# Deferred inverse transforms of eight token tiles, each issued four down matmuls later

## The chip, the cores and the metric

The kernel runs on one core of a Trainium2 chip. The metric is the device time in microseconds (us) of that core, as the median of several executions. A program on one core has no second core to compare its state with, so a run counts as undisturbed when the profile's granted TensorE clock is 1.000 and its time lies within 1.5% of the fastest of the same kernel. "Stage" means one stretch of a trace: from the end of the first block of gate/up matmuls to the start of the second. That is where the change acts.

## The reference

A layer on 2048 tokens of 576 features: a spectral filter (a 2D real FFT, a product with weights, the inverse FFT) added to the input, then a gated feed-forward part added to that.

```python
x = A_x
h = x + irfft2(rfft2(layernorm(x)) * (w_r + 1j * w_i))        # spectral part
n = layernorm(h)
h2 = h + (gelu(n @ w_gate) * (n @ w_up)) @ w_down             # 576 -> 4608 -> 576
```

## The kernel before

Almost all of the work is matmuls, the transforms too. (PSUM is the memory in which matmul results land, in banks; every matmul comes with a load of its weights, "PEld" in the traces.) The kernel has 16 token tiles of 128 tokens, and the feed-forward part goes in four blocks of four tiles: 36 groups of gate/up matmuls (each ends in a GELU on ScalarE and a product on VectorE), then the down matmuls. Only the first eight tiles have their last inverse transform done before the feed-forward part starts. The other eight are "deferred": their transforms are spread among the 288 down matmuls of the first block, whose own tiles don't need them.

A deferred tile has two parts. The first part is eight matmuls into PSUM banks 2 and 3, a ScalarE copy (EB) and four VectorE sums (two into QB, two into YB). The second part is two matmuls on YB into banks 4 and 5, an add onto the residual XO (VectorE) and a sum of squares (ScalarE).

```python
def def_i(c):                                   # "first part"
    ...                                         # 8 matmuls of 144 columns -> banks 2, 3      (L877)
    P.op(ACT, ... activation(EB, bank 2, Copy))                                             # (L880)
    for i, op in enumerate((ALU.add, ALU.subtract)):
        P.op(DVE, ... tensor_tensor(QB[i], bank 3, EB, op))                                 # (L884)
    P.op(DVE, ... tensor_tensor(y2[:, :, 0:HK], QB[:, 0::2, :], QB[:, 1::2, :], add))       # (L886)
    P.op(DVE, ... tensor_tensor(y2[:, ::-1, ...], QB..., QB..., subtract))                  # (L887)

def def_n(c):                                   # "second part"
    ...                                         # 2 matmuls of 288 columns on YB -> banks 4, 5 (L891)
    P.op(DVE, ... tensor_tensor(x2, banks 4 and 5, x2, add))                                # (L894)
    square(c, JD[:, :], "JD")                                                               # (L746)

DSTEP, DLAG = (36, 22) if NPRE == 8 else (28, 22)      # NPRE is 8
for j, c in enumerate(range(NPRE, NT)):
    defer(DSTEP * j, def_i, c)                  # before down matmul number 36 * j
    defer(DSTEP * j + DLAG, def_n, c)           # 22 down matmuls later

def down(tb, p):                                # one token tile, in two halves of 36 matmuls
    for h, (d0, d1) in enumerate(((0, cut), (cut, D))):
        for k, f in enumerate(...):
            if tb == 0:
                for fn in DEF.get(72 * p + 36 * h + k, ()):
                    fn()
            P.op(PE, ... matmul(bank b, AT[:, f, ...], WD[:, f, d0:d1]))                    # (L926)
        P.op(DVE, ... tensor_tensor(OS, bank b, XO, add))      # eviction of the half       # (L929)
```

In the traces here VectorE works in the order in which the program issued its instructions (in the first unit of the stage: lines L848, L884, L886, L887, L894, L929). So where a part is deferred to decides two things: how many down matmuls TensorE can do while VectorE works on the tile, and behind what the tile's VectorE work queues.

## Time and profile before

| kernel before | value |
|---|---|
| time, median of 3 runs (lowest to highest) | 492.3 us (492.15 to 492.36) |
| span of the profiled execution | 490.0 us |
| TensorE busy | 484.2 us, 99% |
| the stage | 129.98 to 171.35, 41.37 us |
| one deferred tile's cadence in it | 5.16 us |

The prediction shows the rows that carry this. One view it only mentions is the busy time of each engine in the stage's first two units. The columns are the stretch, its length, and for each engine the busy time and the number of instructions.

```profile
core 0: us, PE busy (x) PEld busy (x) DVE busy (x) ACT busy (x) POOL busy (x), PEclk, DMA share, GB/s
130.00:135.30 5.30, 5.30 (x50) 4.27 (x51) 3.54 (x7) 1.77 (x4) 0.00 (x0) 1.00 0.02 3
135.30:140.40 5.10, 5.10 (x49) 4.16 (x47) 2.86 (x6) 1.28 (x3) 0.00 (x0) 1.00 0.05 14
```

TensorE (PE) is busy without a gap. VectorE (DVE) works 2.86 us in a usual unit, and 3.54 us in the first, which still has the last product of the gate/up block to do. That product is what the first tile's sums queue behind: they start 1.34 us after the tile's first part (129.98 to 131.32), against 0.73 us in the next unit (135.26 to 135.99).

### The profile page before, as it was taken

The page shows a single profiled execution, that of the slowest core. Times are in us where ns is not written, and L with a number is a line of the kernel's source. Part 1 is how long each engine was busy: PE and PEld are TensorE (multiplying, and loading weights), DVE is VectorE, ACT ScalarE, POOL GpSimd, SP SyncE. Part 2 cuts the span into 40 slices and gives each one's busy share as a digit, 9 for nine tenths or more (in the row PEclk, how much of TensorE's full clock was granted, in tenths as well). Part 3 has the DMA queues.
Part 4 walks back from the last instruction along what each step waited for, and adds up shares of the span by engine and source line. Part 5 has one row for each costly group of instructions (what it writes and reads, how often), then busy time and mean ns, then how long its engine had stood idle before and what let it go on. Part 6 is the DMA issues. An engine that isn't in the chain of part 4 may idle for free.

```text
span 490.0 us, 9898 instructions
## 1 busy us (share of the span) xinstructions
PE 484.2 (99%) x4373; PEld 285.7 (58%) x4374; DVE 190.9 (39%) x381; ACT 150.9 (31%) x291; POOL 33.4 (7%) x61
## 2 busy tenths in 40 slices
PE   7999999999999999999999999999999999999998
PEld 3787754444588744444577644444677544444775
DVE  6999623443455534333311144433211233333111
ACT  6899852233222222322200033233100122323000
POOL 6411541000000020000000000000000000000000
PEclk9999999999999999999999999999999999999999
DMA  8990997211000071100000001000000000000000
GB/s 281 242 324 18 373 372 272 70 25 21 1 14 17 13 233 23 23 4 1 1 18 14 19 18 23 17 0 1 7 19 19 7 0 1 1 1 1 14 19 18
DMA packets 25147, 31.26 MB, mean 64 GB/s; under 512 B 11440, under 2 KB 17840, under 8 KB 25104
## 3 DMA queue, kind: packets, MB, share of 16 engines
q1 hardware_dynamic: 22208, 18.68, 13.1%
q0 software_dynamic: 2896, 11.95, 6.9%
q8 instruction: 34, 0.56, 0.5%
q14 instruction: 9, 0.07, 0.1%
HBM read 26.29 MB, written 2.36 MB: 58 GB/s over the span
## 4 chain that ended last, share of the span: by engine, by line
PE 96%; DVE 1%; DMA 1%; SPq 0%; POOL 0%; issue 0%; POOLq 0%; DVEq 0%
PE PS L839 57%; PE PS L926 29%; PE PS L600 2%; PE PS L610 2%; PE PS L531 1%; PE PS L717 1%; DMA XO<-in_A_x_dram 1%; PE PS L640 1%; PE PS L755 1%; PE PS L877 1%; DVE ST L475 1%; PE PS L891 0%; PE PS L804 0%; SPq L221 0%; DVE VR L655 0%; DVE TP L619 0%
## 5 line engine op out<-in xcount | busy, mean ns | idle before, releaser
L839 PE MATMUL PS<-HT,WG 64*128 64x512 bf16 (+1 forms) x2142 | 228.5, 373 | 0.0
L839 PEld LDWEIGHTS PS<-HT,WG 64*128 64x128 bf16 x2142 | 104.1, 94 | 122.7 <-issue 0.7
L848 DVE TENSOR_TENSOR AT<-GL,PS 128x512 bf16<-128x512 bf16 x144 | 99.0, 688 | 177.5 <-ACT GL L847 177.5
L847 ACT ACTIVATE GL<-PS 128x512 bf16<-128x512 f32 x144 | 85.9, 597 | 262.4 <-PE PS L839 248.9
L926 PE MATMUL PS<-WD,AT 128*128 128x288 bf16 (+2 forms) x1152 | 144.3, 286 | 0.0
L926 PEld LDWEIGHTS PS<-WD,AT 128*128 128x128 bf16 x1152 | 110.7, 98 | 30.8 <-ACT GL L847 1.3
L929 DVE TENSOR_TENSOR OS<-PS,XO 128x288 bf16<-128x288 f32 (+2 forms) x32 | 14.6, 458 | 100.4 <-PE PS L926 100.4
L839 PE MATMUL PS<-HT,WGX 64*128 64x512 bf16 x486 | 53.4, 376 | 0.0
L839 PEld LDWEIGHTS PS<-HT,WGX 64*128 64x128 bf16 x486 | 23.7, 94 | 28.7
L746 ACT ACTIVATE JD<-XO,NM 128x576 bf16<-128x576 bf16 x8 | 6.2, 776 | 28.4 <-DVE XO L894 28.4
L600 PE MATMUL PS<-FT,U 128*128 128x288 bf16 x96 | 14.2, 287 | 0.0
L619 DVE TENSOR_TENSOR TP<-YS,WS 128x1152 bf16<-128x1152 bf16 (+2 forms) x17 | 11.8, 718 | 0.3
L531 PE MATMUL PS<-ATS,XO 128*128 128x128 bf16 (+1 forms) x128 | 10.1, 221 | 1.4 <-POOL XN L545 0.8
L475 DVE BATCH_NORM_STATS2 ST<-XO 128x6 f32<-128x288 bf16 x24 | 9.3, 438 | 4.1 <-DMA XO<-in_A_x_dram 4.1
L600 PEld LDWEIGHTS PS<-FT,U 128*128 128x128 bf16 x96 | 9.2, 98 | 2.4 <-DVE U L540 0.2
L591 ACT ACTIVATE YS<-PS 128x576 bf16<-128x576 f32 x15 | 9.6, 651 | 2.0 <-PE PS L610 1.8
L531 PEld LDWEIGHTS PS<-ATS,XO 128*128 128x128 bf16 (+1 forms) x128 | 7.4, 97 | 4.4 <-POOL XN L545 1.3
L610 PE MATMUL PS<-CUS,BT 128*128 128x288 bf16 x64 | 10.0, 286 | 0.0
L591 ACT ACTIVATE CUS<-PS 128x576 bf16<-128x576 f32 x14 | 9.1, 650 | 0.8 <-PE PS L600 0.4
L894 DVE TENSOR_TENSOR XO<-PS,XO 128x576 bf16<-128x576 f32 x8 | 6.1, 758 | 8.0 <-PE PS L891 8.0
L640 PE MATMUL PS<-VT,ZS 128*128 128x256 bf16 x64 | 8.8, 273 | 0.3 <-DVE ZS L630 0.3
L591 ACT ACTIVATE V<-PS 128x512 bf16<-128x512 f32 (+1 forms) x17 | 9.0, 582 | 0.0
(79 smaller groups left out, 210.2 us busy)
## 6 DMA issues: line engine op xcount, KB each, us to landing
WD<-in_B_w_down_dram POOLq DMA_DIRECT2D x9, 576.0 KB, 10.7
WG<-in_B_w_up_dram SPq DMA_DIRECT2D x4, 1152.0 KB, 6.9
WG<-in_B_w_gate_dram POOLq DMA_DIRECT2D x4, 1152.0 KB, 9.7
out_dram<-OS SPq DMA_DIRECT2D x30, 72.0 KB, 1.6
XO<-in_A_x_dram SPq DMA_DIRECT2D x3, 576.0 KB, 7.0
WGX<-in_B_w_up_dram SPq DMA_DIRECT2D x1, 1152.0 KB, 6.0
WGX<-in_B_w_gate_dram POOLq DMA_DIRECT2D x1, 1152.0 KB, 9.9
HT<-HN SPq DMA_TRANSPOSE x60, 2.4
```

The source lines that it names most:

```text
L475: P.op(DVE, lambda v, c=c, h=h: v.bn_stats(ST1[:, c, h, :], XO[:, c, 288 * h:288 * h + 288]), r=[("X", c)], w=[("ST1", c, h)])
L531: P.op(PE, lambda t, b=b, lhs=lhs, p0=p0, p1=p1, s=s, e=e, o=o, c=c: t.matmul(bank(b, p0, p1, o, o + 128), lhs, ATS[:, c, :], start=s, sto ...
L591: fn = (lambda v: v.tensor_copy(dst, src)) if eng == DVE else (lambda a: a.activation(dst, src, ACTF.Copy))
L600: P.op(PE, lambda t, b=b, m=m, us=us, o=o, g=g: t.matmul(bank(b, 0, 128, 0, 2 * HK), U[:, us, g, :, :], FT[:, 3 * o + (2 if us == 4 else u ...
L610: P.op(PE, lambda t, b=b, tb=tb, m=m, s3=s3, sp_=sp_: t.matmul(bank(b, 0, 128, 0, KW), BT[:, sp_, tb, :], CUS[:, s3, m, :], start=(m == 0) ...
L619: P.op(DVE, lambda v: v.tensor_tensor(TP[:, sl, :, :, q0:q1], y4, w4, op=ALU.mult), r=[("Y", sl), ("Wn", i)] + (wkeys[0] if 1 <= g < 9 els ...
L640: P.op(PE, lambda t, b=b[c], c=c, zp=zp, sp_=sp_, z3=z3: t.matmul(bank(b, 0, 128, 256 * c, 256 * c + 256), ZS[:, z3, zp, c:256:2], VT[:, s ...
L839: op = P.op(PE, lambda t, h0=h0, kt=kt, wt=wt, b=b, s=(not second and j == 0), e=(second and j == n - 1): t.matmul(bank(b, 0, 128, c0, c1) ...
L847: P.op(ACT, lambda a: a.activation(GL[:, s2, :], bank(b0), ACTF.Gelu_apprx_tanh), r=[("PS", b0)], w=[("GL", s2)])
L848: P.op(DVE, lambda v: v.tensor_tensor(AT[:, f, :], GL[:, s2, :], bank(b0 + 1), op=ALU.mult), r=[("GL", s2), ("PS", b0 + 1)], w=[("AT", f)])
L926: P.op(PE, lambda t, b=b, d0=d0, d1=d1, f=f, p=p: t.matmul(bank(b, 0, 128, 0, d1 - d0), AT[:, f, 128 * p:128 * p + 128], WD[:, f, d0:d1], ...
L929: P.op(DVE, lambda v, b=b, d0=d0, d1=d1, p=p, c=c: v.tensor_tensor(OS[:, p % 2, d0:d1], bank(b, 0, 128, 0, d1 - d0), XO[:, c, d0:d1], op=A ...
```

## The change

The intent, as I read it, is slack. Each deferred tile keeps its distance of 22 down matmuls between its parts, but both parts come four down matmuls later. So the first tile's VectorE work no longer meets the end of the gate/up block quite as closely.

```diff
     for j, c in enumerate(range(NPRE, NT)):
-        defer(DSTEP * j, def_i, c)
-        defer(DSTEP * j + DLAG, def_n, c)
+        defer(DSTEP * j + 4, def_i, c)
+        defer(DSTEP * j + DLAG + 4, def_n, c)
     if NPRE < 8:
         ...                                     # t2 gets + 4 too; not taken: NPRE is 8
```

More of the change, by code (lines that the diff above doesn't have):

```diff
@@ L907, in _build @@
     for j, c in enumerate(range(NPRE, NT)):
-        defer(DSTEP * j, def_i, c)
-        defer(DSTEP * j + DLAG, def_n, c)
+        defer(DSTEP * j + 4, def_i, c)
+        defer(DSTEP * j + DLAG + 4, def_n, c)
     if NPRE < 8:
-        t2 = DSTEP * (8 - NPRE) + DLAG
+        t2 = DSTEP * (8 - NPRE) + DLAG + 4
         defer(t2 - 14, ln2_late, 3)
```

## The prediction

> **What bounds the kernel now.** I read the page first, for which engine the span is made of:
>
> ```profile
> span 490.0 us, 9898 instructions
> ...
> PE 484.2 (99%) x4373; PEld 285.7 (58%) x4374; DVE 190.9 (39%) x381; ACT 150.9 (31%) x291; POOL 33.4 (7%) x61
> ...
> PE 96%; DVE 1%; DMA 1%; SPq 0%; POOL 0%; issue 0%; POOLq 0%; DVEq 0%
> ```
>
> TensorE is busy for 99% of the span, at a clock that is never throttled (the view of the cores gives a mean granted clock of 1.000), and 96% of the chain that ended last is TensorE. But the page says of itself that a busy TensorE is not one at its peak, so a waiting matmul could hide in that 99%. What counts is the cadence of the matmuls in the stage that the change touches. So the second view is that chain in order of time, around the first block of down matmuls (source line 926), where the eight deferred tiles are worked off: L877 is the first matmul group of a deferred inverse transform (eight matmuls, I call it "first part"), L891 the second (two matmuls, "second part"), L839 the gate/up matmuls on either side.
>
> ```profile
> 129.98 0.61 PE PS L877 x8
> 130.59 2.69 PE PS L926 x22
> 133.55 1.72 PE PS L926 x14
> 135.26 0.50 PE PS L877 x8
> 135.76 2.69 PE PS L926 x22
> 138.70 1.72 PE PS L926 x14
> ...
> 171.35 70.04 PE PS L839 x648
> 241.38 35.39 PE PS L926 x288
> ```
>
> The columns are start, duration (us), then engine, tile, line and count. The reader is to see a strict repeat. A unit is 8 first-part matmuls, 22 down, 2 second-part (0.24 to 0.26 us, too short to be listed here), 14 down, and the next unit starts 5.16 us later; there is no row of anything but TensorE between 129.98 and 171.35. Waits are the third view, limited to this stage. For TensorE itself it lists nothing, for its weight loads two rows, and the other engines wait for TensorE:
>
> ```profile
> DVE XO L894 <- PE PS L891: 8.0, 8, 1.1
> DVE OS L929 <- PE PS L926: 7.9, 8, 1.0
> ACT EB L880 <- PE PS L877: 2.1, 7, 0.3
> ...
> DVE QB L884 <- ACT EB L880: 1.4, 7, 0.2
> PEld PS L877 <- issue: 0.4, 1, 0.4
> PEld PS L839 <- issue: 0.2, 1, 0.2
> ```
>
> The two weight-load rows are the two changes of matmul kind at the stage's ends. They happen once each. So the stage runs at TensorE's rate, and everything on VectorE and ScalarE lies beside it.
>
> **What the Trainium skill says.** "TensorE: Matmul & The Clock Gate", section "Wait — 56ns, not 53.3ns?", gives for a warm stream a start-to-start of N / 2.4 GHz plus about 2.5 ns. Worked out (an estimate from that page): 122.5 ns for the 288 columns of a down or second-part matmul, 62.5 ns for the 144 columns of a first-part one. The trace agrees to the last digit it shows: 36 down matmuls in 2.69 + 1.72 = 4.41 us are 122.5 ns each, and eight first-part ones in 0.50 us are 62.5 ns each. So the formula is a usable zero line, and whatever a stage takes above it is what better placing could win. "PSUM — Partial Sum Buffer", section "PSUM bank collisions raise a hardware error", asks that PSUM be guarded by bank; this matters here because a moved matmul could be made to wait for a bank. By the source the down matmuls of this block use banks 0 and 1 (6 and 7 for the last tile), the first part 2 and 3, the second 4 and 5. The trace agrees that none is waited for: no TensorE wait row in the stage. "Trainium Architecture — The Big Picture", section "What this means for kernel authors", has the engines as independent processors that meet only at semaphores; the trace agrees, with TensorE continuous while VectorE works about 2.9 us of each 5.16 us unit.
>
> **The change part by part.** It removes nothing and adds nothing: same 288 down, 64 first-part and 16 second-part matmuls, same copies and adds. It moves every first part from just ahead of a half's first down matmul to after four of them, and every second part from after 22 to after 26. The 22 down matmuls between a tile's two parts stay 22. (The branch for fewer than eight early tiles isn't taken: the kernel has eight.)
>
> The ceiling of a gain. Zero line of the stage by the two rates: 288 x 122.5 ns + 64 x 62.5 ns + 16 x 122.5 ns = 35.28 + 4.00 + 1.96 = 41.24 us. Measured: 171.35 - 129.98 = 41.37 us. Only 0.13 us is there to be won. Of it 0.11 us is the first unit's first group, 0.61 us where the others take 0.50: the change from gate/up to full-height matmuls. The change keeps that, it only falls on a down matmul: where a later block goes from gate/up straight to down matmuls, its 288 take 35.39 us, that is 35.39 - 35.28 = 0.11 us over. That leaves 0.02 us, and it can be found. In the first unit L926 starts at 130.59 and resumes at 133.55, 2.96 us; in the next 135.76 to 138.70, 2.94 us. The detailed timeline says why:
>
> ```profile
> 130.58 0.41 ACT L880 ACTIVATE EB<-PS 128x288 f32<-128x288 f32 x1
> 130.72 0.69 DVE L848 TENSOR_TENSOR AT<-GL,PS 128x512 bf16<-128x512 bf16 x1 [0.18 <-ACT GL L847]
> 131.32 0.81 DVE L884 TENSOR_TENSOR QB<-PS,EB 128x288 f32<-128x288 f32 x2
> 132.17 0.46 DVE L886 TENSOR_TENSOR YB<-QB 128x288 bf16<-128x288 f32 x1
> 132.54 0.45 DVE L887 TENSOR_TENSOR YB<-QB 128x288 bf16<-128x288 f32 x1
> 133.11 0.13 PEld L891 LDWEIGHTS PS<-YB,ITD 128*128 128x128 bf16 x2
> ```
>
> The first tile's VectorE chain queues behind the last gate product (L848), ends at 132.99, and TensorE wants its result at 133.11: just in time. This is surely what the change is after. Four down matmuls (0.49 us) later, the chain still starts near 131.3 (it waits for that same product), so it ends near 133.0, while its user comes at about 133.6. Slack grows from about 0.1 to 0.6 us, and 0.02 us of time is won. For the seven other tiles the whole chain moves along with its own matmuls: in the last, L887 ends at 168.61 and the second part's load starts at 169.10, so its slack of about 0.5 us stays.
>
> Costs at the other end. The stage's last second part is followed by 10 down matmuls instead of 14, so its residual add (169.67 for 0.76 us), its square and the GpSimd statistics run 0.49 us later. The add would end at 170.92, still ahead of the last down eviction at 171.45. The statistics now end at 171.71 + 1.65 = 173.36, then at about 173.85; their first user, the normalisation of tile 8, starts at 177.69, after a gate product that it queues behind. The weights loaded into the space freed here are issued at 172.31 to 174.2 and land at most 10.4 us later; the first matmul to use them loads at 222.66. A slip of 0.5 us against 3.8 and 38 us costs nothing. Sum: -0.02 + 0 = -0.02 us, on 492.3.
>
> **The rivals.** First, that the move collides on VectorE: the eviction of a finished half (L929, 0.46 us at 135.30) ran between one tile's add and the next tile's first sum. In the changed order the add ends 0.49 us nearer to it (134.34 + 0.49 = 134.83, still 0.47 us before), and the next sum starts later (135.99 + 0.49), further from it. If they did collide, a tile's chain would slip by at most 0.46 us, against its slack of 0.5; even all eight going 0.1 us past it would cost 0.8 us, 0.2%. Second, that the move takes a real stall out of every half boundary, because a down bank or a deferred bank is held there. For: that is where the change is made. Against: the groups of eight take 0.50 us, which is exactly their rate, and the down groups too. It would need 1.2 us a boundary to make 2%, and the excess of the whole stage is 0.13 us. Third, that ScalarE delays the chain: its square (134.38 to 135.25) ends 0.30 us before the next tile's copy at 135.55; both shift together, so that gap stays. Fourth, a slip at the stage's end that delays the weight load of a later block: it would have to be 38 us.
>
> **Range and chances.** The prediction is the time before, 492.3 us, as 0.02 us is below its last digit. Three runs before spread over 0.2 us; a repetition, another instruction layout or a chip warmed otherwise may shift by about twice that, which is my choice for the range: 491.9 to 492.7. For a change of 2% (9.8 us) the eight units would each have to move by 1.2 us, a quarter of their length, and no rival comes near. I give 1% to either side for what I haven't seen.
>
> **What would show it right or wrong.** Right: from the end of the first gate/up block to the start of the second still 41.3 to 41.4 us; first groups of down matmuls now 4 then 22 then 10 long; first-part groups at 0.50 us, all of them; the extra 0.11 us now on the first four down matmuls (about 0.60 us); the second part's first load with an idle gap of nothing, and the VectorE chain of the first tile ending about 0.6 us before it; no TensorE wait row. Wrong: a row of VectorE or ScalarE in the chain between 130 and 172 us, a TensorE wait for YB, EB or an XO add, or units longer than 5.16 us. It would also be wrong by a clock granted below 1.0, which nothing here would cause.

## The result, and the profile after

The changed kernel takes 492.26 us (median of 6 runs, 492.17 to 492.33) beside 492.23 us for the kernel before (6 runs, 491.98 to 492.6); 492.3 was predicted. The ratio is 1.0, with a 95% interval of 0.9988 to 1.0013.

The whole page first: the profiled span is 490.2 us instead of 490.0.

```profile
span 490.2 us, 9899 instructions
...
PE 483.9 (99%) x4373; PEld 285.7 (58%) x4374; DVE 191.0 (39%) x381; ACT 151.0 (31%) x291; POOL 33.4 (7%) x61
```

The 0.2 us aren't the change's. The chain that ended last, in order of time, has its first large row here for the kernel before:

```profile
2.12 5.44 DMA XO<-in_A_x_dram
```

and here for the changed one:

```profile
2.12 5.61 DMA XO<-in_A_x_dram
```

The load of the input took 0.17 us longer in this execution, 120 us before the first changed instruction, and all that follows is late by it or by 0.02 us more. Comparing times of day between the two traces therefore needs an offset of 0.19 us at the stage's start (129.98 against 130.17). Durations need none. The same chain in the stage of the changed kernel:

```profile
130.17 0.60 PE PS L926 x4
130.77 0.50 PE PS L877 x8
131.27 2.69 PE PS L926 x22
...
134.21 1.72 PE PS L926 x14
135.92 0.50 PE PS L877 x8
136.42 2.69 PE PS L926 x22
...
170.29 1.23 PE PS L926 x10
171.52 70.04 PE PS L839 x648
```

The stage is 171.52 - 130.17 = 41.35 us, against 41.37: the 0.02 us that was forecast. The groups of 22, of 14 and of 8 take what they took. The first four down matmuls carry the 0.11 us for changing over from gate/up matmuls (0.60 us in place of 0.49), which the first eight L877 carried before. The last group of the stage is 10 long, as the second part moved toward the stage's end. The first unit in detail shows the slack:

```profile
130.90 0.69 DVE L848 TENSOR_TENSOR AT<-GL,PS 128x512 bf16<-128x512 bf16 x1 [0.17 <-ACT GL L847]
131.05 0.41 ACT L880 ACTIVATE EB<-PS 128x288 f32<-128x288 f32 x1 [0.18 <-PE PS L877]
131.50 0.82 DVE L884 TENSOR_TENSOR QB<-PS,EB 128x288 f32<-128x288 f32 x2
132.73 0.45 DVE L887 TENSOR_TENSOR YB<-QB 128x288 bf16<-128x288 f32 x1
133.68 0.22 PEld L891 LDWEIGHTS PS<-YB,ITD 128*128 128x128 bf16 x2
133.80 0.41 PE L891 MATMUL PS<-YB,ITD 128*128 128x288 bf16 x2
```

These are selected rows. The tile's first sum (L884) starts at 131.50, which is 1.33 us after the stage's start; before it was 131.32 - 129.98 = 1.34 us. The four down matmuls ahead of the first part have not delayed it, because it was waiting on VectorE for L848 anyway. They take up just that wait: the copy now ends at 131.05 + 0.41 = 131.46, 0.04 us before the first sum. Its last sum ends at 133.18, and the weight load of the second part comes at 133.68. Before, the two were at 132.99 and 133.11, with the load held back. The last tile's slack is 0.50 us as well (169.26 to 169.76), so the change has brought the first tile level with the others.

### The profile page after: what moved, and what is told of

Read it like the earlier page. It is cut to its first block, busy times and chain, and to the rows that moved or that the text cites. A ratio compares the mean times of both kernels' runs of the same rounds, so it can differ in the third digit from the quotient of the medians.

```text
span 490.2 us, 9899 instructions
## 1 busy us (share of the span) xinstructions
PE 483.9 (99%) x4373; PEld 285.7 (58%) x4374; DVE 191.0 (39%) x381; ACT 151.0 (31%) x291; POOL 33.4 (7%) x61
## 4 chain that ended last, share of the span: by engine, by line
PE 96%; DVE 1%; DMA 1%; SPq 0%; POOL 0%; issue 0%; POOLq 0%; DVEq 0%
PE PS L839 57%; PE PS L926 29%; PE PS L600 2%; PE PS L610 2%; PE PS L531 1%; PE PS L717 1%; DMA XO<-in_A_x_dram 1%; PE PS L640 1%; PE PS L755 1%; PE PS L877 1%; DVE ST L475 1%; PE PS L891 0%; PE PS L804 0%; SPq L221 0%; DVE VR L655 0%; DVE TP L619 0%
## 5 line engine op out<-in xcount | busy, mean ns | idle before, releaser
L848 DVE TENSOR_TENSOR AT<-GL,PS 128x512 bf16<-128x512 bf16 x144 | 99.0, 688 | 177.4 <-ACT GL L847 177.4
```

The source lines that it names most:

```text
L848: P.op(DVE, lambda v: v.tensor_tensor(AT[:, f, :], GL[:, s2, :], bank(b0 + 1), op=ALU.mult), r=[("GL", s2), ("PS", b0 + 1)], w=[("AT", f)])
```

## The experiments

Times with rounds come from two groups of four kernels, each with its own runs of the kernel before on the same chip: 492.16 us in the first group, 492.25 us in the second. In some of these traces the chain leaves TensorE in the first unit. There the stage's start is read as the start of the block's last GELU less 0.10 us, which is its place in the other traces (for example 130.27 against 130.17 in the changed kernel; 0.11 in the kernel before), so such a stage is good to about 0.01 us.

**How long may a tile take? The second parts sooner.** With the first parts as in the kernel before, the distance is 6 instead of 22. My theory is that TensorE sets the stage and placement is free as long as a tile's chain of sums ends in time; the rival is that chain or load give way.

```diff
-        defer(DSTEP * j + DLAG, def_n, c)
+        defer(DSTEP * j + 6, def_n, c)
```

> First parts as in the kernel before, second parts 6 down matmuls after them. My theory: a second part is due 1.24 us after the first part's start (1.35 in the first unit) but can run at 2.72 (3.31) us, so TensorE stalls 1.48 us in each of seven units and 1.96 us in the first: 12.3 us in all, stage about 53.6 us, time about 504.6 us, 2.5% slower. The rival that the chain gets shorter when TensorE is idle, or that the weight load ahead of the matmul hides more: less than 10 us.

It took 504.01 us, ratio 1.0239 (1.0224 to 1.0254). The chain in order of time, one unit in the middle and the end:

```profile
137.47 0.26 PE PS L877 x4
137.76 0.42 ACT EB L880
...
139.51 0.38 DVE YB L887
...
139.94 0.42 PE PS L891 x2
140.36 3.67 PE PS L926 x30
144.03 0.26 PE PS L877 x4
...
183.42 6.58 PE PS L839 x59
```

Now ScalarE and VectorE are in the chain: the tile's copy and sums set the cadence. The stage is 183.42 - 130.23 = 53.19 us, 11.82 us longer than that of the kernel before (12.3 was expected; the rival with less than 10 us is out), and the time is 11.85 us above the kernel before: what the stage loses, the kernel loses in full. A unit of the seven later ones takes (183.42 - 137.47) / 7 = 6.56 us, 1.41 us over 5.155 (36 + 2 matmuls of 122.5 ns and 8 of 62.5 ns), where 1.48 was expected. The second part was due 1.24 us after its first part's start, so it can run 1.24 + 1.41 = 2.65 us after it. With 22 it is due at 0.50 + 22 x 0.1225 = 3.20 us. **The reserve of the seven later units is 0.55 us**, some four and a half down matmuls.

**At the edge, with and without the moved first part.** The distance is 18 in both of these; in the second, the first parts stand four later, as in the change.

```diff
-        defer(DSTEP * j, def_i, c)
-        defer(DSTEP * j + DLAG, def_n, c)
+        defer(DSTEP * j + 0, def_i, c)          # the other kernel: + 4
+        defer(DSTEP * j + 18, def_n, c)         # the other kernel: + 22
```

> First parts where the kernel before has them, second parts 18 down matmuls after them in place of 22. My theory: TensorE stalls only where a tile's VectorE chain ends too late for its second part; from the two traces a second-part matmul runs 0.30 us after the chain's last write at the earliest, the chain ends 3.01 us after the block's start in the first unit and 2.42 us after the first part's start in the others. So the first unit loses 3.31 - 2.81 = 0.50 us, the seven others 2.72 - 2.70 = 0.02 us each; the stage from the first to the second gate/up block goes from 41.37 to about 41.95 us, the time to about 492.8 us. The rival, that the units have a large hidden reserve and the placement is free: stage 41.35 us, time 492.3. The rival that the eviction or the square collides with the chain: stalls in all units, stage above 43 us.

> Only the first part of the change: first parts four down matmuls later, second parts where the kernel before has them (18 after the first part). My theory: the first unit's chain still ends 3.01 us after the block's start (it waits there for the last gate product), but its second part is due 3.31 us after it, so it loses about 0; the other units 0.02 us each; stage about 41.5 us, time about 492.4 us. That is some 0.45 us less than with the same 18 and the first parts not moved: the slack that the change buys, made visible. Rival, that the four matmuls give the first unit no slack: the same stage as that kernel, 41.95 us or more.

The first took 492.68 us (1.0011, 0.9995 to 1.0028), the second 492.14 us (0.9999, 0.9984 to 1.0014); the intervals overlap, so the traces decide. The first kernel's stage is 171.93 - 130.08 = 41.85 us, with waits of TensorE for the chain in the first unit alone. The 0.02 us expected of each other unit did not come, as the reserve of 0.55 us covers the 0.49 us taken away. The waits are these (in brackets the engine's idle time before the row, in us, and what ended it):

```profile
133.20 0.13 PEld L891 LDWEIGHTS PS<-YB,ITD 128*128 128x128 bf16 x2 [0.63 <-issue]
133.24 0.40 PE L891 MATMUL PS<-YB,ITD 128*128 128x288 bf16 x2 [0.35 <-DVE YB L887]
```

The second's is 171.74 - 130.37 = 41.37 us, and the profile lists no wait of TensorE in it, though the load comes only 0.03 us before its matmul:

```profile
133.50 0.13 PEld L891 LDWEIGHTS PS<-YB,ITD 128*128 128x128 bf16 x2
133.53 0.41 PE L891 MATMUL PS<-YB,ITD 128*128 128x288 bf16 x2
```

So **moving the first part gives the first unit 0.48 us of reserve** (41.85 - 41.37), four down matmuls' worth. With 22 no one uses it. The second kernel is as tight in its first unit as the kernel before was: the same 0.03 us, the same stage of 41.37 us.

**Both parts as late as they go.** Thirteen later in place of four; the second part is then the last but one thing in its half.

```diff
-        defer(DSTEP * j, def_i, c)
-        defer(DSTEP * j + DLAG, def_n, c)
+        defer(DSTEP * j + 13, def_i, c)
+        defer(DSTEP * j + DLAG + 13, def_n, c)
```

> Both parts 13 down matmuls later than in the kernel before, gap of 22 kept: the second part is now one down matmul before the half's end, so its residual add (0.76 us) and the half's eviction (0.46 us) meet on VectorE. My theory: the eviction waits some 0.6 us, nothing waits for it within 36 down matmuls, and the stage stays 41.35 us; the statistics at the stage's end slip by 1.6 us against the 0.5 of the change and are still in time; time 492.3 us. Rival, a collision on VectorE that reaches TensorE: up to 0.46 us a unit, stage up to 45 us, time up to 496 us.

It took 492.29 us (1.0, 0.9985 to 1.0015), its stage 171.63 - 130.28 = 41.35 us. The residual add and the eviction do meet on VectorE:

```profile
135.46 0.76 DVE L894 TENSOR_TENSOR XO<-PS,XO 128x576 bf16<-128x576 f32 x1 [1.06 <-PE PS L891]
136.13 0.45 DVE L929 TENSOR_TENSOR OS<-PS,XO 128x288 bf16<-128x288 f32 x1
```

The eviction follows the add without a gap, it started 136.13 - 135.46 = 0.67 us after the add did, and the stage did not grow. The collision was real and free, so this rival is out for the change's four as well. The first tile's slack is 0.50 us here too (its sums end at 134.39, the load comes at 134.89): by this reading, moving further than four buys no more.

**Only the second part moved.** The first parts stay at the half's boundary, the second parts come 26 after.

```diff
-        defer(DSTEP * j + DLAG, def_n, c)
+        defer(DSTEP * j + 26, def_n, c)
```

> Only the second part of the change: second parts 26 down matmuls after the first ones, which stay where the kernel before has them. My theory: every unit gets 0.49 us more reserve, none is used but the 0.02 us of the first; stage 41.35 us, time 492.2 us, same as the change. Rival, that the first part's place at a half's boundary costs something that the change took away: stage 41.37 us or more.

It took 492.05 us (1.0004, 0.9987 to 1.002), its stage 171.10 - 129.76 = 41.34 us. The 0.02 us are won as well, so, as far as one trace of each can tell, moving the first part off the boundary wins nothing of its own.

**A longer chain, in both orders.** One of the two last sums is done three times over; the result stays right.

```diff
         P.op(DVE, ... tensor_tensor(y2[:, :, 0:HK], QB..., QB..., add))
+        P.op(DVE, ... tensor_tensor(y2[:, :, 0:HK], QB..., QB..., add))
+        P.op(DVE, ... tensor_tensor(y2[:, :, 0:HK], QB..., QB..., add))
```

> The kernel before, with one of a tile's VectorE sums done three times: its chain gets two steps of 0.38 us longer, 0.76 us. My theory, with the reserve as the kernels with 6 and 18 in place of 22 showed it (a second part can run 2.65 us after its first part's start and is due at 3.20 us; in the first unit it is due just when it can run): seven units lose 0.76 - 0.55 = 0.21 us, the first 0.76 us and more or less 0.02; the stage goes from 41.37 to about 43.6 us, the time to about 494.4 us. Rival, that VectorE's own load is what counts and not the chain: nothing below 5 us of VectorE work a unit, stage 41.37 us.

> The changed kernel with the same two extra sums. My theory: the seven later units lose 0.21 us each as without the change, the first 0.76 - 0.49 = 0.27 us; stage about 43.1 us, time about 493.9 us, some 0.5 us less than the same chain in the order before. Rival, that the change gives every tile 0.49 us of reserve and not only the first: about 0 lost in all units, stage 41.4 us, time 492.2 us.

They took 496.12 us (1.0078, 1.0063 to 1.0094) and 495.37 us (1.0066, 1.0051 to 1.0081), both more than expected. Stages: 175.08 - 129.70 = 45.38 us and 174.63 - 129.74 = 44.89 us. The first of them, from the chain in order of time and, for the four sums, from the timeline:

```profile
135.96 0.26 PE PS L877 x4
...
137.54 0.46 DVE L886 TENSOR_TENSOR YB<-QB 128x288 bf16<-128x288 f32 x1
138.04 0.46 DVE L887 TENSOR_TENSOR YB<-QB 128x288 bf16<-128x288 f32 x1
138.53 0.46 DVE L888 TENSOR_TENSOR YB<-QB 128x288 bf16<-128x288 f32 x1
138.90 0.45 DVE L889 TENSOR_TENSOR YB<-QB 128x288 bf16<-128x288 f32 x1
...
175.08 3.12 PE PS L839 x27
```

The second kernel's stage, from its chain:

```profile
129.74 0.60 PE PS L928 x4
...
174.63 3.56 PE PS L839 x31
```

The two added lines shift the line numbers: L889 is the last sum here, L928 the down matmul. Mis-sized was the extra step. The first three sums write the same half of YB, and the program makes each wait for the one before: 0.49 us from start to start. The fourth writes the other half and follows 0.37 us after the third. So the chain grew by 2 x 0.49 = 0.98 us, not 0.76. Less the reserve of 0.55 us this gives 0.43 us lost in each later unit; measured are (175.08 - 135.96) / 7 - 5.155 = 0.43 us. The reserve holds. Between the two stages lie 0.49 us, again in the first unit: a later unit loses 0.43 us in both orders. So the rival that each tile gained reserve is out, and so is the one that only VectorE's load counts (at some 3.8 us a unit it stayed below 5 us, and the stage still grew by 4.01 us). The times alone would not settle the difference of the orders, as their intervals overlap.

**Less matmul work.** A wrong result: half of each first part is left out of the changed kernel.

```diff
-                for i, ch in enumerate((o, 2)):
+                for i, ch in enumerate((o,)):
...
-                                 start=(i == 0), stop=(i == 1)),
+                                 start=(i == 0), stop=True),
```

> A wrong result on purpose: the changed kernel with half of each first part left out (4 matmuls of 144 columns in place of 8, without the third group of frequencies). My theory that the stage is the sum of its matmuls: 32 matmuls of 62.5 ns less, 2.0 us, stage 39.35 us, time about 490.2 us. Rival, that something beside TensorE holds the stage at 41.35 us and the placement didn't matter for that reason: time 492.2 us.

It took 489.99 us (0.9958, 0.9943 to 0.9972). (The record marks its output as correct all the same; how strict that check is isn't on record, and the run is used for its time alone.) Its chain:

```profile
129.90 0.60 PE PS L926 x4
...
169.24 8.95 PE PS L839 x81
```

The stage is 169.24 - 129.90 = 39.34 us, 2.01 us less for 32 matmuls less of 62.5 ns. Nothing beside TensorE holds the stage up at 41.35 us. Of all that was tried, only less work on TensorE made it shorter by more than 0.03 us.

## Why the prediction was right

- **The bound.** TensorE's own rate sets the stage. Shown: 32 matmuls less took 2.01 us off the stage, and where TensorE had to wait for the tiles' sums (6 in place of 22) the stage grew by 11.82 us and the time by 11.85 us.
- **The zero line.** The sum of 41.24 us plus 0.11 us for the change of matmul kind is 41.35 us. The changed kernel's stage, and that of the kernel with both parts 13 later, is 41.35 us.
- **The ceiling and the 0.02 us.** The gain in the stage was 41.37 - 41.35 = 0.02 us, in the first unit. In the times it can't be seen: the runs of the kernel before alone spread over 0.6 us. It is a reading of traces. The kernels with the same stage agree with it, but each of them is one trace.
- **The first tile's slack.** Here a size was off: 0.6 us was predicted, 133.68 - 133.18 = 0.50 us was measured. The chain was placed rightly (at 133.0, plus the offset of 0.19). The term that failed is its user "at about 133.6": it added 0.49 us to the load at 133.11, but that load had been held back by the chain. A weight load that isn't held starts 0.12 us ahead of its matmul's record (133.68 and 133.80), the held one 0.03 us ahead (133.11 and 133.14, in the kernel before). The reserve before was nothing, not 0.1 us. The view of waits, on which the prediction relied, does not list so short a hold.
- **The other tiles' slack** of about 0.5 us stayed; their reserve by the kernels with 6 and with the longer chain is 0.55 us. (Slack is read in one trace, from the end of the last sum to the load; reserve is what can be taken away before the stage grows.)
- **The collision on VectorE.** As predicted, in the changed kernel the add ended 135.47 - 135.00 = 0.47 us ahead of the eviction; driven to a real collision, it cost nothing.
- **The boundary as a stall.** Predicted as absent; moving the second part alone gave the same stage.
- **ScalarE's square and the stage's end.** The next copy still came 0.30 us after the square's last instruction (135.91 to 136.21). The statistics ended at 174.02 us; less the offset at the stage's end of 0.17 us (171.35 against 171.52) that is 173.85, as predicted. Their first user came at 177.86, that is 177.69 as before, and the first matmul on the later block's weights loaded them at 222.83 (222.66 before).
- **The signs named beforehand.** They came, but for one: after the second part the groups of down matmuls are 14 long and not 10, because the last 10 of a half and the first 4 of the next now follow each other. Only the stage's last group is 10.

What stays open: why the waiting load came 0.12 us after the last sum in the first unit and sooner in later ones (see the last section); and whether 0.02 us is a real gain in the mean of many runs. Nothing here could measure that, and I see no use that would follow from it.

## What to carry to other kernels

Where an engine is saturated without a gap, compute its zero line from instruction counts and the measured rate before moving anything: the excess over it, here 0.13 us of 41.37, is the most that a better order of the same work can win. As long as reserve is left, moving work that lies beside the bound changes reserve, not time; find the reserve by shortening the distance until the stage grows. Reserve is still worth something where a later change will lengthen the chain: with 0.98 us more in the chain, the changed order lost 0.49 us less in the stage.

## What the Trainium skill lacked or had wrong

- "TensorE: Matmul & The Clock Gate" (the table at its head) says that weight loads are pulled ahead of running matmuls, but not how far, nor what a late one costs. In these traces a free load starts 0.12 us ahead of its matmul's record; one that was held to 0.03 us ahead cost the stream only 0.02 us.
- "TensorEngine Tiling (Array Packing)", section "Key Properties", says that changing the tiling mode drains TensorE and gives no figure. Going from the 64-row gate/up matmuls to the full-height ones cost 0.11 us here, whichever kind of full-height matmul came first.
- "VectorE: DVE Perf Modes", section "The DRAIN you can't avoid", reports that a semaphore after each operation cost nothing extra in its measurement (it also says that an operation which is not held starts earlier). Here a sum that waited for the one before it, as both write the same half of YB, started 0.49 us after it, and one that didn't wait 0.37 us after: the wait cost 0.12 us.
- No page that I read gives the time from a VectorE result to a matmul that waits for it. Here the waiting weight load started 0.12 us after the last sum's end in the first unit of the kernel before (132.99 to 133.11), but 0.06 us after it in the later units that wait (139.88 to 139.94 in the kernel with 6, 139.35 to 139.41 with the longer chain). By the source the first of these loads also checks for its table ITD; whether that is the difference was not tested.
